# Turning the first expert item's first 256 rows: from TensorE transposes in query tiles 6 to 9 to VectorE in tiles 11 to 17

## Chip, cores, metric

One Trainium2 chip, one of its cores. The metric is device time of one execution in microseconds (us); a time of a kernel is the median of several executions.

## What is computed

Linear attention with positive random features (4 batches, 8 heads, 576 positions, head width 64, 128 features), and on its output a top-1 mixture of 8 experts over 2304 rows of 512 columns:

```python
def phi(x):                                   # x scaled by D ** -0.25
    h = x @ omega.T - sum(x * x) / 2
    return exp(h - max(h)) / sqrt(m)
q_p, k_p = phi(q), phi(k)
kv, z = k_p.T @ v, sum(k_p)                   # per batch and head
x = (q_p @ kv) / (q_p @ z + 1e-6)             # -> rows of 512
logits = x @ w_gate; e = argmax(logits)       # one expert a row, at most `capacity` rows each
out = gate * (relu(x @ w1[e]) @ w2[e])        # rows of an expert, 576 slots
```

All is float32. The expert products are made of split operands: `hi` is a value rounded to the matmul's reduced type, `lo` the rest, and hi*hi, hi*lo and lo*hi are added.

## The kernel before

The order on every engine is the order of the source: one loop (`for n in range(NK + NT + 3)`) runs over 18 groups of keys and then over query tiles, `t = n - NK`, of 128 rows. In query tile t:

- TensorE projects the queries of tile t on the features (`pjq`, L175), transposes the features of tile t - 2 (`qtr`, L782: two row halves of the array work side by side, 8 transposes each), and multiplies the transposed features of tile t - 3 with `kv_sb` into the PSUM pair `qacc` (`numer`, L654). From t = 18 on there is no projection; tiles 18 and 20 put `qacc` into other banks than the pair.
- VectorE takes the maxima `mx` of tile t's projection, half of them from PSUM (`pjq`) and half from the copy `d` (L192), and normalises tile t - 3 (`normalise`: `den`, `rec`, `xr`, `lg`, L678 to L685).
- GpSimd adds the maxima to half of `d` (L837); ScalarE does the copy, the other half and the exponentials `qpT`.
- SP's queue writes the finished rows `xr` to DRAM (`x_d`, L686) and loads queries (`load_q`, three tiles at a time, two buffers) and weights.

Beside this, generators in `tasks` advance at marks: `run("P")` lets `first_splits` do up to two steps of splitting the first item's `w1` on GpSimd (one `w1hi` of 128x1024, or one of four `w1lo` of 128x256, for each of four chunks), `run("E")` at a tile's end lets `first_item` issue a weight load. The first item (the first batch's expert) needs its 576 rows column-major, as `xhi` and `xlo`. Rows 256 to 575 are read back from `x_d` (`first_rows` in tile 15) and turned on VectorE in tiles 18 and 19 (`turn_x`, 32x32 block transposes). Rows 0 to 255 take another way: GpSimd copies the two finished tiles into `xt` (L690), TensorE transposes 64 rows in each of tiles 6 to 9 among the `qtr` (four `xtri` transposes of 64x128 a tile), ScalarE casts the result to `xhi` (L430) and VectorE subtracts to `xlo` (L432). The first expert matmul, `mm1(0, 0)`, follows `numer` in tile 20; it and the next five use rows 0 to 255 alone, then rows 256 on.

Of the kernel before, what the change touches and what calls it, by code (L numbers as in the profile page):

```python
# [19 lines left out]
B, H, S, D, M = 4, 8, 576, 64, 128  # L20
N, DM, E, FF = B * S, H * D, 8, 1024
NP = H // 2
NT = N // 128
# [13 lines left out]
AHEAD = [(0, 0)]  # L37
NJ = 11
FIRST_LOAD = 15
W1_LOADS = (0, 6, 9, 12)  # L40
W2_LOADS = 16
FIRST_AT = (6, 7, 8, 9)
BRANCH_AT = 4
EPS = 1e-6 * M
BIG = 1048576.0
# [18 lines left out]
def attention_moe(ctx, tc, kT, qT, va, om, wg, w1, w2, cap, ident, tri, desc, lst, tab0, out):  # L64
# [13 lines left out]
    def bank(i, name):  # L78
        return ps.tile([128, 512], F32, tag=f"b{i}", name=name, bufs=1)
# [68 lines left out]
    def start(gen):  # L148
        tasks.append([gen, None])
# [7 lines left out]
    def run(at=None, times=1, most=99):  # L157
        for _ in range(times):
            for task in list(tasks):
                if task[1] is None or (task[1] == at and most > 0):  # L160
                    most -= task[1] is not None
                    run_one(task)
# [9 lines left out]
    def project(parts, banks):  # L172
        def one(k, i):
            rows = slice(64 * i, 64 * i + 64)
            nc.tensor.matmul(banks[i][:, k * M : (k + 1) * M], parts[k][rows, :], om_s[rows, :], start=True, stop=True)  # L175

        a = 0
        if beside:
            a, small_t = beside.pop(0)
            small_t()  # L180
        n = len(parts)
        one(0, 1 - a)
        for k in range(1, n):
            one(k - 1, a)
            one(k, 1 - a)
        one(n - 1, a)
# [208 lines left out]
                in_offset=bass.IndirectOffsetOnAxis(ap=big["idx"][0:n, i, 2:3], axis=0),  # L395
            )

    def load_x(rows, b0=0):
        src = x_d[rows, :].rearrange("(b r) (q c) -> q r b c", r=32, q=4)
        for q in range(4):  # L400
            nc.sync.dma_start(big["xz"][32 * q : 32 * q + 32, b0:, :], src[q])


    def turn_x(b0, b1, o=0, eng=nc.vector):
        t = big["xt"][:, o : o + b1 - b0, :].rearrange("p b (k r) -> p b k r", k=4)
        nc.vector.transpose(t, big["xz"][:, b0:b1, :].rearrange("p b (a k) -> p b k a", k=4))
        t = t.rearrange("p b k r -> p k b r")
        hi, lo = (big[x][:, :, 32 * b0 : 32 * b1].rearrange("p k (b r) -> p k b r", r=32) for x in ("xhi", "xlo"))

        def split():  # L410
            nc.scalar.copy(hi, t)
            eng.tensor_tensor(lo, t, hi.bitcast(F32), op=ALU.subtract)

        return split

    def transpose_x(i, nm, at):
        n = sub_n[i]
# [186 lines left out]
    def first_item():  # L604
        yield from pause(6)
        e0 = const.tile([1, E + 2], F32, name="e0")
        e0i = const.tile([1, 1], I32, name="e0i")
        lg0 = lg[0:1, 0, :]
        nc.vector.tensor_reduce(e0[:, E : E + 1], lg0, op=ALU.max, axis=AX.X)
        yield  # L610
        nc.vector.scalar_tensor_tensor(
            e0[:, 0:E], lg0, e0[:, E : E + 1], desc_sb[0:1, :], op0=ALU.is_ge, op1=ALU.mult
        )
        yield
        nc.vector.tensor_reduce(e0[:, E + 1 : E + 2], e0[:, 0:E], op=ALU.max, axis=AX.X)
        yield
        nc.vector.tensor_scalar(e0i, e0[:, E + 1 : E + 2], -1.0, float(E), op0=ALU.mult, op1=ALU.add)
        yield
        ev = nc.sync.value_load(e0i[0:1, 0:1], min_val=0, max_val=E - 1)
        for c in range(4):  # L620
            while step[0] < W1_LOADS[c]:
                yield "E"
            load_w(1, c, ev)
            if c == 1:
                start(first_splits())
            yield "E"
        while step[0] < W2_LOADS:
            yield "E"
        for c in range(4):
            load_w(2, c, ev)  # L630
            yield "E"
# [9 lines left out]
                split_w_lo(1, c, nc.gpsimd, k)  # L641

    xr_l = {}

    def first_rows():
        load_x(slice(32 * NBA, SLOTS), NBA)
# [15 lines left out]
    def normalise(t, acc, whole):  # L664
        xr = small.tile([128, ROW, H], F32, tag="xr", name=f"xr{t}", bufs=3)
        av = [acc_i[:, 0 : NP * ROW].rearrange("p (h c) -> p c h", c=ROW) for acc_i in acc]
        if whole is not None:
            av = [whole.rearrange("p (i x) -> p i x", i=2)[:, :, 0 : NP * ROW].rearrange("p i (h c) -> p c i h", c=ROW)]
        n = len(av)
        den = small.tile([128, H], F32, tag="den", name=f"den{t}")  # L670
        rec = small.tile([128, H], F32, tag="rec", name=f"rec{t}")

        def heads(x, i, pat):
            x = x[..., i * NP : (i + 1) * NP] if n > 1 else x
            return x if n > 1 else x.rearrange(pat, i=2)

        for i in range(n):
            nc.vector.tensor_scalar(heads(den, i, "p (i h) -> p i h"), av[i][:, D], EPS, None, op0=ALU.add)  # L678
        nc.vector.reciprocal(rec, den)
        for i in range(n):  # L680
            r = heads(rec, i, "p (i h) -> p i h").unsqueeze(1)
            nc.vector.tensor_tensor(
                heads(xr, i, "p c (i h) -> p c i h"), av[i], r.to_broadcast([128, ROW, *r.shape[2:]]), op=ALU.mult
            )
        nc.vector.tensor_reduce(lg[:, t, :], xr[:, D + 1 : ROW, :], op=ALU.add, axis=AX.X)  # L685
        nc.sync.dma_start(x_d[t * 128 : (t + 1) * 128, :], xr[:, 0:D, :].rearrange("p c h -> p (c h)"))  # L686
        if t < 2:

            xr_l[t] = big["xt"][:, 4 * t : 4 * t + 4, :]
            nc.gpsimd.tensor_copy(xr_l[t], xr[:, 0:D, :].rearrange("p c h -> p (c h)").rearrange("p (m k) -> p k m", k=4))  # L690

    HALVES = [(0, 256), (256, SLOTS)]

# [42 lines left out]
    for n in range(NK + NT + 3):  # L736
# [3 lines left out]
        if n < NK:  # L740
            keys = [chunks[b, g][0][:, u * 128 : (u + 1) * 128] for b, g, u in KU[KG * n : KG * n + KG]]
            if n == 0:

                pj = [bank(i, f"pjk{n}{i}") for i in range(4)]
                project(keys[0:2], pj[0:2])
                project(keys[2:4], pj[2:4])
            else:

                if n == 1:
                    pj = [bank(SM, "pjk10"), pair("pjk11")[:, 0:512]]  # L750
                else:
                    pj = [bank(2 * (n % 2) + i, f"pjk{n}{i}") for i in range(2)]
                project(keys, pj)
        elif t < NT:
            pj = [bank((2 * t + i) % 3, f"pjq{n}{i}") for i in range(2)]
            c = max(i for i in range(len(QB) - 1) if QB[i] <= t)
            o = (t - QB[c]) * 128
            project([qc[c][:, p, o : o + 128] for p in range(NP)], pj)
        run("T")

        if 0 <= t - 2 < NT:
            d = d_l.pop(t - 2)
            trs = [bank((3 + i, (2, SM)[i])[t > NT], f"qtr{n}{i}") for i in range(2)]

            parts = [
                [(trs[i][:, u * 64 : (u + 1) * 64], d[64 * i : 64 * i + 64, u, :], i) for u in range(H)] for i in range(2)
            ]

            if t in FIRST_AT:
                k0 = FIRST_AT.index(t)  # L770
                i = k0 % 2
                tr = bank(SM, f"xtri0{k0}")
                rows = slice(64 * i, 64 * i + 64)
                x0 = xr_l[k0 // 2]
                parts[i][0:0] = [
                    (tr[:, k * 64 : (k + 1) * 64], x0[rows, k, :], i) for k in range(4)
                ]
                start(copy_x(tr, 64 * k0, 64))
            for x in chain(*zip_longest(*parts)):
                if x is not None:  # L780
                    rows = slice(64 * x[2], 64 * x[2] + 64)
                    nc.tensor.transpose(x[0], x[1], id_sb[rows, rows])  # L782
# [47 lines left out]
        else:  # L830
            if t < NT:
# [4 lines left out]
                maxima(mx, 0, d[:, 0:4, :])  # L836
                nc.gpsimd.tensor_tensor(d[:, 0:4, :], d[:, 0:4, :], spread(mx, 0), op=ALU.add)  # L837
                d_l[t] = d
            run("P", times=2, most=2)
            if 0 <= t - 2 < NT:  # L840
                qpT = qp.tile([128, 2, H * 64], F32, tag="qpT", name=f"qpT{t}", bufs=2)
                for i in range(2):
# [15 lines left out]
            if 0 <= t - 3 < NT:  # L858
                normalise(t - 3, acc_l[0], whole)
                if t == 3:  # L860
                    start(first_item())
            if t in (NT, NT + 1):

                b0 = NBA + 5 * (t - NT)
                split_x = turn_x(b0, b0 + 5, b0 - NBA, nc.gpsimd)
            run(times=3)
        if 0 <= t < NT and t - QB[c] == 2 and c + 2 < len(QB) - 1:
            load_q(c + 2)
        run("E")

        if n == NK + 1:
# [2 lines left out]
        if n < NK:  # L874

            for k in range(KB, 2 * B):
                if (9 * (k - KB) + 8) // KG + 2 == n:
                    load_k(k // 2, k % 2)
            if n == 3:
                start(setup())  # L880
            if n in (NK - 4, NK - 2):
                load_q(0 if n == NK - 4 else 1)
        if t == FIRST_LOAD:
            first_rows()
    qstack.close()
# [317 lines left out]
```

## Time and profile before

| what | value |
|---|---|
| time, median of 3 runs | 261.43 us (260.79 to 261.9) |
| the profiled execution's own time | 260.95 us |
| its span, first to last instruction | 259.2 us |
| TensorE (PE) busy | 253.7 us, 98% |
| VectorE (DVE) busy | 167.2 us, 65% |
| ScalarE (ACT) busy | 148.8 us, 57% |
| GpSimd (POOL) busy | 42.6 us, 16% |

Busy shares are means over the whole span. The key stage runs up to 46 us, the query tiles to about 101, the expert stage behind them. PE's weight loads (PEld) overlap its matmuls and stand apart. SPq is the queue from which SP issues DMAs.

### The profile page before, as it was taken

The page shows a single profiled execution, that of the slowest core. Times are in us where ns is not written, and L with a number is a line of the kernel's source. Part 1 is how long each engine was busy: PE and PEld are TensorE (multiplying, and loading weights), DVE is VectorE, ACT ScalarE, POOL GpSimd, SP SyncE. Part 2 cuts the span into 40 slices and gives each one's busy share as a digit, 9 for nine tenths or more (in the row PEclk, how much of TensorE's full clock was granted, in tenths as well). Part 3 has the DMA queues.
Part 4 walks back from the last instruction along what each step waited for, and adds up shares of the span by engine and source line. Part 5 has one row for each costly group of instructions (what it writes and reads, how often), then busy time and mean ns, then how long its engine had stood idle before and what let it go on. Part 6 is the DMA issues. An engine that isn't in the chain of part 4 may idle for free. (4 is left out here: it accounts for less than half of the span.)

```text
span 259.2 us, 7581 instructions
## 1 busy us (share of the span) xinstructions
PE 253.7 (98%) x3058; PEld 232.7 (90%) x3058; DVE 167.2 (65%) x351; ACT 148.8 (57%) x374; POOL 42.6 (16%) x61
## 2 busy tenths in 40 slices
PE   7999999999999999999999999999999999999994
PEld 6999999999999999999988789999888999998882
DVE  3999888779999998655763745566850064667500
ACT  3788888899999995326402536552361155524611
POOL 1002000255369896200000000000000000000000
PEclk9999999999999999999999999999999999999999
DMA  7999870034976769990059619992012897950121
GB/s 204 390 382 349 285 254 3 5 122 149 311 234 207 275 169 289 373 390 21 1 134 276 206 49 311 213 286 66 3 40 66 293 245 206 326 164 0 49 93 48
DMA packets 35171, 48.54 MB, mean 187 GB/s; under 512 B 2290, under 2 KB 23410, under 8 KB 35122
## 3 DMA queue, kind: packets, MB, share of 16 engines
q1 hardware_dynamic: 34002, 46.39, 57.0%
q10 hardware_dynamic: 1120, 1.52, 1.9%
q8 instruction: 28, 0.46, 0.7%
q14 instruction: 21, 0.17, 0.2%
HBM read 35.97 MB, written 11.93 MB: 185 GB/s over the span
## 5 line engine op out<-in xcount | busy, mean ns | idle before, releaser
L705 PE MATMUL hi<-xhi,w1hi 128*128 128x256 f32 (+1 forms) x192 | 56.7, 295 | 0.0
L706 PE MATMUL hi<-xhi,w1lo 128*128 128x256 f32 (+1 forms) x192 | 56.4, 294 | 0.0
L707 PE MATMUL hi<-xlo,w1hi 128*128 128x256 f32 (+1 forms) x192 | 56.3, 293 | 0.0
L718 DVE SCALAR_TENSOR_TENSOR hlo<-hi,hhi 128x256 fp32r<-128x256 f32 x48 | 20.2, 420 | 44.4 <-ACT hhi L716 22.4
L716 ACT ACTIVATE hhi<-hi 128x256 fp32r<-128x256 f32 x48 | 18.3, 384 | 36.1 <-PE hi L707 36.1
L898 PE MATMUL yi<-w2hi,hhi 128*128 128x512 f32 x96 | 37.5, 390 | 0.3 <-issue 0.3
L899 PE MATMUL yi<-w2hi,hlo 128*128 128x512 f32 x96 | 37.4, 389 | 0.0
L705 PEld LDWEIGHTS hi<-xhi,w1hi 128*128 128x128 f32 x192 | 36.0, 188 | 0.3
L706 PEld LDWEIGHTS hi<-xhi,w1lo 128*128 128x128 f32 x192 | 36.0, 188 | 0.1
L707 PEld LDWEIGHTS hi<-xlo,w1hi 128*128 128x128 f32 x192 | 36.0, 187 | 0.0
L192 DVE TENSOR_REDUCE mx<-pjk 128x4 f32<-128x512 f32 (+1 forms) x38 | 23.4, 656 | 4.2 <-PE pjk L175 4.0
L837 POOL TENSOR_TENSOR d<-d,mx 128x512 f32<-128x512 f32 x18 | 18.7, 1039 | 42.2 <-DVE mx L192 39.8
L175 PE MATMUL pjk<-om_s,kraw 64*128 64x128 f32 x288 | 23.9, 300 | 0.2
L818 ACT ACTIVATE ex<-pjk,mx 128x128 f32<-128x128 f32 x72 | 20.6, 368 | 6.0 <-DVE mx L192 5.7
L904 PE MATMUL yi<-w2lo,hhi 128*128 128x512 f32 x96 | 23.7, 389 | 0.0
L654 PE MATMUL qacc<-kv_sb,qpT 128*64 128x73 f32 x576 | 22.5, 230 | 0.1
L898 PEld LDWEIGHTS yi<-w2hi,hhi 128*128 128x128 f32 x96 | 18.0, 188 | 4.3 <-issue 0.7
L175 PEld LDWEIGHTS pjk<-om_s,kraw 64*128 64x128 f32 x288 | 20.4, 203 | 1.5 <-DMA kraw<-kT 0.6
L175 PE MATMUL pjq<-om_s,qraw 64*128 64x128 f32 x288 | 21.6, 284 | 0.0
L904 PEld LDWEIGHTS yi<-w2lo,hhi 128*128 128x128 f32 x96 | 18.0, 188 | 3.7
L899 PEld LDWEIGHTS yi<-w2hi,hlo 128*128 128x128 f32 x96 | 18.0, 188 | 3.6
L852 ACT ACTIVATE d<-pjq,mx 128x128 f32<-128x128 f32 x72 | 21.0, 404 | 0.3 <-DVE mx L192 0.3
(148 smaller groups left out, 416.4 us busy)
## 6 DMA issues: line engine op xcount, KB each, us to landing
w1raw<-w SPq DMA_DIRECT2D x16, 512.0 KB, 6.8
w2raw<-w SPq DMA_DIRECT2D x16, 512.0 KB, 5.8
qraw<-qT SPq DMA_DIRECT2D x6, 768.0 KB, 6.3
x_d<-xr SPq DMA_DIRECT2D x18, 256.0 KB, 4.3
v<-va SPq DMA_DIRECT2D x7, 650.0 KB, 6.5
xg<-x_d SPq DMA_DIRECT2D x12, 288.0 KB, 7.6
kraw<-kT SPq DMA_DIRECT2D x5, 576.0 KB, 7.0
out<-ysi SPq DMA_DIRECT2D x9, 256.0 KB, 2.1
```

The source lines that it names most:

```text
L175: nc.tensor.matmul(banks[i][:, k * M : (k + 1) * M], parts[k][rows, :], om_s[rows, :], start=True, stop=True)
L192: nc.vector.tensor_reduce(mx[:, a : a + src.shape[1]], src, op=ALU.max, axis=AX.X, negate=True)
L654: nc.tensor.matmul(acc[i][r : r + 64, p * ROW : (p + 1) * ROW], qpT[:, r // 64, (4 * i + p) * 64 : (4 * i + p) * 64 + 64], kv_sb[(t * 128 ...
L705: nc.tensor.matmul(pt, whi_[:, k, fs], xhi[:, k, sl], start=(k == 0), stop=False)
L706: nc.tensor.matmul(pt, wlo_[:, k, fs], xhi[:, k, sl], start=False, stop=False)
L707: nc.tensor.matmul(pt, whi_[:, k, fs], xlo[:, k, sl], start=False, stop=(k == 3))
L718: nc.vector.scalar_tensor_tensor(lo, src, 0.0, hi.bitcast(F32), op0=ALU.max, op1=ALU.subtract)
L818: nc.scalar.activation(ex[:, o + k, :], q[0][:, k * M : (k + 1) * M], AF.Exp, bias=mx[:, o + k : o + k + 1], scale=1.0)
L852: nc.scalar.activation(d[:, 4 + k, :], pj[1][:, k * M : (k + 1) * M], AF.Identity, bias=mx[:, 4 + k : 5 + k], scale=1.0)
L898: nc.tensor.matmul(pt, hhi[:, f, sl], w2_at(w_hi, f), start=(f == 0), stop=False)
L899: nc.tensor.matmul(pt, hlo[:, f, sl], w2_at(w_hi, f), start=False, stop=False)
L904: nc.tensor.matmul(pt, hhi[:, f, sl], w2_at(w_lo, f), start=False, stop=(f == 7))
```

## The change

Rows 0 to 255 are now read back from `x_d` at the end of tile 5 (four loads of 32 partitions x 8 blocks). In tiles 11 to 16 VectorE turns one block of 32 rows each, in tile 17 two; in tiles 12, 14, 16 and 17 GpSimd casts two blocks to `xhi` and subtracts to `xlo`. The TensorE transposes, the ScalarE casts, the VectorE subtractions and the GpSimd copies of those rows are gone. The splitting of `w1` starts when its first chunk's load is issued, not the second's, and takes one step a tile in tiles 11 to 15. A query load is issued right behind the projection that frees its buffer, not at the tile's end.

```diff
+EARLY_LOAD = 5
+EARLY = {11 + i: (i, i + 1 + (i == 6)) for i in range(7)}
-FIRST_AT = (6, 7, 8, 9)
...
+    def split_early(t):
+        b0, b1 = EARLY[t - (t < max(EARLY))][0], EARLY[t][1]
+        x = big["xt"][:, b0:b1, :].rearrange("p b (k r) -> p k b r", k=4)
+        hi, lo = (big[n][:, :, 32 * b0 : 32 * b1].rearrange("p k (b r) -> p k b r", r=32) for n in ("xhi", "xlo"))
+        split_hi(hi, x, nc.gpsimd)
+        split_lo(lo, x, hi, nc.gpsimd)
...
             load_w(1, c, ev)
-            if c == 1:
+            if c == 0:
                 start(first_splits())
...
-        if t < 2:
-            xr_l[t] = big["xt"][:, 4 * t : 4 * t + 4, :]
-            nc.gpsimd.tensor_copy(xr_l[t], xr[:, 0:D, :].rearrange("p c h -> p (c h)").rearrange("p (m k) -> p k m", k=4))
...
             project([qc[c][:, p, o : o + 128] for p in range(NP)], pj)
+            if t - QB[c] == 2 and c + 2 < len(QB) - 1:
+                load_q(c + 2)
...
-            if t in FIRST_AT:
-                k0 = FIRST_AT.index(t)
-                i = k0 % 2
-                tr = bank(SM, f"xtri0{k0}")
-                rows = slice(64 * i, 64 * i + 64)
-                x0 = xr_l[k0 // 2]
-                parts[i][0:0] = [
-                    (tr[:, k * 64 : (k + 1) * 64], x0[rows, k, :], i) for k in range(4)
-                ]
-                start(copy_x(tr, 64 * k0, 64))
...
-            run("P", times=2, most=2)
+            run("P", times=2, most=1 if 11 <= t <= 15 else 2)
...
+            if t in EARLY:
+                turn_x(*EARLY[t], EARLY[t][0])
+                if t % 2 == 0 or t == max(EARLY):
+                    split_early(t)
...
-        if 0 <= t < NT and t - QB[c] == 2 and c + 2 < len(QB) - 1:
-            load_q(c + 2)
...
+        if t == EARLY_LOAD:
+            load_x(slice(0, 32 * NBA), 0, NBA)
```

VectorE, from the maxima of tile 11 to those of tile 12 (`mx30` and `d12` are tile 12's, `den8` and `xr8` normalise tile 8). Before:

```order
L192 TENSOR_REDUCE mx29_1670<-d11_1716 128x4
L678 TENSOR_SCALAR den8_1731<-qacc11_1699 128x8
L679 RECIPROCAL rec8_1732<-den8_1731 128x8
L682 TENSOR_TENSOR xr8_1730<-qacc11_1699,rec8_1732 128x584
L685 TENSOR_REDUCE lg_86<-xr8_1730 128x8
L192 TENSOR_REDUCE mx30_1740<-pjq301_1742 128x4
L192 TENSOR_REDUCE mx30_1740<-d12_1786 128x4
```

The same place on VectorE in the changed kernel:

```order
L193 TENSOR_REDUCE mx29_1650<-d11_1698 128x4
L684 TENSOR_SCALAR den8_1712<-qacc11_1681 128x8
L685 RECIPROCAL rec8_1713<-den8_1712 128x8
L688 TENSOR_TENSOR xr8_1711<-qacc11_1681,rec8_1713 128x584
L691 TENSOR_REDUCE lg_86<-xr8_1711 128x8
L407 STREAM_TRANSPOSE xt_1008<-xg_1007 128x128
L193 TENSOR_REDUCE mx30_1720<-pjq301_1722 128x4
L193 TENSOR_REDUCE mx30_1720<-d12_1766 128x4
```

One instruction came in between `lg` and the next maxima; the same holds in tiles 12 to 16.

GpSimd, from the step on `d16` to the end of the splits (`w1hi3` and `w1lo3` are the fourth chunk of w1). Before:

```order
L837 TENSOR_TENSOR d16_2063<-d16_2063,mx34_2017 128x512
L140 TENSOR_TENSOR w1lo2_1000<-w1raw2_992,w1hi2_996 128x256
L135 TENSOR_SCALAR w1hi3_997<-w1raw3_993 128x1024
L837 TENSOR_TENSOR d17_2132<-d17_2132,mx35_2086 128x512
L140 TENSOR_TENSOR w1lo3_1001<-w1raw3_993,w1hi3_997 128x256 x4
```

The same place on GpSimd in the changed kernel:

```order
L831 TENSOR_TENSOR d16_2047<-d16_2047,mx34_2001 128x512
L136 TENSOR_SCALAR w1hi3_997<-w1raw3_993 128x1024
L141 TENSOR_TENSOR w1lo3_1001<-w1raw3_993,w1hi3_997 128x256
L136 TENSOR_SCALAR xhi_1009<-xt_1008 128x4x64
L141 TENSOR_TENSOR xlo_1010<-xt_1008,xhi_1009 128x4x64
L831 TENSOR_TENSOR d17_2119<-d17_2119,mx35_2073 128x512
L141 TENSOR_TENSOR w1lo3_1001<-w1raw3_993,w1hi3_997 128x256 x2
L136 TENSOR_SCALAR xhi_1009<-xt_1008 128x4x64
L141 TENSOR_TENSOR xlo_1010<-xt_1008,xhi_1009 128x4x64
L141 TENSOR_TENSOR w1lo3_1001<-w1raw3_993,w1hi3_997 128x256
```

Four instructions stand between d16 and d17 where two stood, and a second pair for `xhi` and `xlo` came in behind d17.

SP's queue, from the load of w1's first chunk to that of its second (`qraw3` holds the queries of tiles 9 to 11, `xr2` is tile 2's rows). Before:

```order
L376 DMA w1raw0_990<-w1 128x4x256
L686 DMA x_d_68<-xr1_1218 128x512
L686 DMA x_d_68<-xr2_1289 128x512
L209 DMA qraw3_1297<-qT 128x4x384
L686 DMA x_d_68<-xr3_1369 128x512
L376 ISA
L376 DMA w1raw1_991<-w1 128x4x256
```

The same place on SP in the changed kernel:

```order
L377 DMA w1raw0_990<-w1 128x4x256
L692 DMA x_d_68<-xr1_1217 128x512
L210 DMA qraw3_1239<-qT 128x4x384
L692 DMA x_d_68<-xr2_1289 128x512
L402 DMA xg_1007<-x_d_68 32x8x128 x4
L692 DMA x_d_68<-xr3_1366 128x512
L377 ISA
L377 DMA w1raw1_991<-w1 128x4x256
```

The query load moved one place ahead, and four loads of the finished rows stand ahead of tile 3's write and w1's second chunk.

## Rows read from the trace of the kernel before

**Rows 1.** Busy by stretch: length, PE, PEld, DVE, ACT, POOL, clock, DMA.

```profile
65.24:68.25 3.01, 3.01 (x73) 2.86 (x69) 2.73 (x8) 2.81 (x9) 0.68 (x2) 1.00 0.89 280
79.83:82.59 2.76, 2.76 (x68) 2.61 (x65) 2.54 (x6) 2.59 (x9) 2.68 (x3) 1.00 0.51 188
101.51:255.40 153.89, 153.58 (x926) 139.46 (x924) 80.96 (x164) 61.73 (x126) 3.15 (x2) 1.00 0.56 166
```

**Rows 2.** Timeline of PE's weight loads, tiles 7 and 12: start, length, instruction.

```profile
66.13 0.14 PEld L782 LDWEIGHTS xtri<-id_sb,xt 64*128 64x128 f32 x1
...
67.07 1.10 PEld L654 LDWEIGHTS qacc<-kv_sb,qpT 128*64 128x64 f32 x32
...
80.71 0.63 PEld L782 LDWEIGHTS qtr<-id_sb,d 64*128 64x128 f32 x16
81.41 1.10 PEld L654 LDWEIGHTS qacc<-kv_sb,qpT 128*64 128x64 f32 x32
```

**Rows 3.** Instructions on the tile xtri: ns min/median/max, first and last start.

```profile
L432 DVE TENSOR_TENSOR xlo<-xtri,xhi x4: 414/414/416, 64.7 to 73.9; 128x256 fp32r<-128x256 f32 x4
```

**Rows 4.** Timeline of VectorE in tile 12.

```profile
79.95 0.17 DVE L678 TENSOR_SCALAR den<-qacc 128x8 f32<-128x8 f32 x1
...
80.39 0.77 DVE L682 TENSOR_TENSOR xr<-qacc,rec 128x584 f32<-128x584 f32 x1
...
81.32 0.68 DVE L192 TENSOR_REDUCE mx<-pjq 128x4 f32<-128x512 f32 x1
81.92 0.68 DVE L192 TENSOR_REDUCE mx<-d 128x4 f32<-128x512 f32 x1
82.71 0.17 DVE L678 TENSOR_SCALAR den<-qacc 128x8 f32<-128x8 f32 x1
```

**Rows 5.** Groups by shape, line 406: count, busy us, mean ns, idle before.

```profile
L406 DVE STREAM_TRANSPOSE xt<-xg 128x1280 f32<-128x1280 f32 x3 | 7.3, 2440 | 0.0
L406 DVE STREAM_TRANSPOSE xt<-xg 128x1024 f32<-128x1024 f32 x3 | 5.9, 1980 | 5.7 <-DMA xg<-x_d 5.7
L406 DVE STREAM_TRANSPOSE xt<-xg 128x640 f32<-128x640 f32 x2 | 2.8, 1388 | 0.0
```

**Rows 6.** Timelines of VectorE and GpSimd, 98.5 to 105 us.

```profile
102.66 1.35 DVE L406 STREAM_TRANSPOSE xt<-xg 128x640 f32<-128x640 f32 x1
...
102.25 1.57 POOL L412 TENSOR_TENSOR xlo<-xt,xhi 128x640 fp32r<-128x640 f32 x1 [1.97 <-ACT xhi L411]
```

**Rows 7.** Timeline of GpSimd; in brackets the idle time before.

```profile
89.20 1.05 POOL L135 TENSOR_SCALAR w1hi<-w1raw 128x1024 fp32r<-128x1024 f32 x1
90.33 0.73 POOL L140 TENSOR_TENSOR w1lo<-w1raw,w1hi 128x256 fp32r<-128x256 f32 x1
...
93.71 1.04 POOL L837 TENSOR_TENSOR d<-d,mx 128x512 f32<-128x512 f32 x1 [0.28 <-DVE mx L192]
...
96.48 1.04 POOL L837 TENSOR_TENSOR d<-d,mx 128x512 f32<-128x512 f32 x1
97.48 2.79 POOL L140 TENSOR_TENSOR w1lo<-w1raw,w1hi 128x256 fp32r<-128x256 f32 x4
```

**Rows 8.** Timeline of PE's weight loads in tile 19, and the first expert matmul.

```profile
98.39 0.57 PEld L782 LDWEIGHTS qtr<-id_sb,d 64*128 64x128 f32 x16
...
101.51 0.19 PEld L705 LDWEIGHTS hi<-xhi,w1hi 128*128 128x128 f32 x1
```

**Rows 9.** SP's issues in time; us to landing: median of x_d, range of w1raw.

```profile
61.34 2.38 SPq L686 DMA_DIRECT2D x_d<-xr  x2
...
67.29 0.58 SPq L376 DMA_DIRECT2D w1raw<-w  x1
...
92.60 1.99 SPq L401 DMA_DIRECT2D xg<-x_d  x4
...
x_d<-xr SPq DMA_DIRECT2D x18, 256.0 KB, 4.3
...
DMA to landing us min/median/max: 4.3/6.8/10.4
```

More of the change, by code (lines that the diff above doesn't have):

```diff
@@ L396, in gather, with load_x @@
             )
-    def load_x(rows, b0=0):
+    def load_x(rows, b0=0, b1=NB):
         src = x_d[rows, :].rearrange("(b r) (q c) -> q r b c", r=32, q=4)
         for q in range(4):
-            nc.sync.dma_start(big["xz"][32 * q : 32 * q + 32, b0:, :], src[q])
+            nc.sync.dma_start(big["xz"][32 * q : 32 * q + 32, b0:b1, :], src[q])
     def turn_x(b0, b1, o=0, eng=nc.vector):
@@ L641, in first_splits @@
                 split_w_lo(1, c, nc.gpsimd, k)
-    xr_l = {}
     def first_rows():
```

## Prediction

> **What bounds the kernel now.** I read the busy time by stretch first. TensorE is busy 2.76 us of a query tile of 2.76 us, and 153.58 us of the 153.89 us from the first expert matmul to its end, at the full granted clock [rows 1]. So the time is TensorE's work. Whatever starts the expert matmuls earlier or later, at 101.51 us [rows 8], moves the end by as much; only the query tiles change here. Second, inside a tile I read TensorE's weight loads, which mark where each group of its instructions starts [rows 2]; third, VectorE's timeline in the same tile [rows 4], because two of its results come back to TensorE: `xr` frees the PSUM pair into which the next tile's `qacc` goes, and `mx` opens the way to `d` on GpSimd. VectorE is nearly full too: 2.54 us of 2.76 [rows 1]. GpSimd shows 2.68 us there, but that is w1 splitting that nobody waits for yet.
>
> **The sum, part by part.**
>
> *Transposes off TensorE.* In tile 12 the step from the first `qtr` load to the first `qacc` load is 81.41 - 80.71 = 0.70 us; in tile 7, with four `xtri` transposes among them, 67.07 - 66.13 = 0.94 [rows 2]. Four tiles carry them: 4 x 0.24 = 0.96 us saved. ScalarE's four casts and VectorE's four subtractions go as well (0.41 us each for VectorE [rows 3]). They ran beside TensorE's longer tile, and without them tile 12 already runs at TensorE's own 2.76 us, so they add nothing to the 0.96.
>
> *The turn on VectorE.* From `den` to the next `den` VectorE takes 82.71 - 79.95 = 2.76 us, TensorE's period. It could do it faster: `mx` to `mx` is 81.92 - 81.32 = 0.60, so after the second `mx` it is free at 82.52 and stands 0.19 us until `qacc` is done. Its own cycle is thus 2.57 us [rows 4]. Each of tiles 11 to 16 now adds one 128x128 STREAM_TRANSPOSE, which no row shows. From the three sizes that it does show, 640, 1024 and 1280 columns in 1388, 1980 and 2440 ns [rows 5], the bounds are: from below in proportion to the largest, 2440/10 = 0.24 us; from above by the line through the smallest and the largest (1.64 ns a column, 336 ns fixed), 0.55 us. Through 1024 and 1280 alone it is 0.37. I take 0.42, between the two lines. Back to back, an instruction of 0.68 us was followed after 0.60, so 0.08 comes off: 0.34. The cycle becomes 2.57 + 0.34 = 2.91, or 0.15 over TensorE's 2.76. Who waits: TensorE's next `qacc`, for `xr`. In tile 12 `xr` ends at 80.39 + 0.77 = 81.16 and `qacc` starts at 81.41 [rows 2, 4]; with about 0.1 for the signal, 0.15 us is spare. The turns of tiles 11 to 15 hold back `qacc` in tiles 13 to 17; tile 18's `qacc` uses other banks, so the turns of tiles 16 and 17 hold back none. That is 5 x 0.15 - 0.15 = 0.60 us given back. At 0.24 us a turn the cycle is 2.73 and nothing is given back; at 0.55 it is 3.04 and 5 x 0.28 - 0.15 = 1.25 is.
>
> [...]
>
> *Splits on GpSimd.* Most of it is covered: the w1 splitting starts three tiles earlier and is thinned to one step a tile in tiles 11 to 15, and `d` is used two tiles after it is made. The end isn't. In tile 16, between d16 and d17, GpSimd now has w1hi3, a w1lo, xhi and xlo. Start to start: d 97.48 - 96.48 = 1.00; hi 90.33 - 89.20 = 1.13; each lo 2.79/4 = 0.69 [rows 7]. The new xhi cast has 256 columns: 0.26 us in proportion to the 1.05 of 1024 columns, at most the 0.73 of a subtraction of the same size; I take 0.40 and 0.08 for its result. Together 1.00 + 1.13 + 0.69 + 0.48 + 0.69 = 3.99 us, where d17 now follows d16 after 96.48 - 93.71 = 2.77. So d17 comes 1.2 us later. It was done at 96.48 + 1.04 = 97.52 and TensorE asks for it at 98.39 [rows 7, 8]: 0.87 us of cover. That leaves a stall of 0.35 to 0.45 in tile 19. VectorE's new lateness within a tile (the 0.19 of idle time that it loses, and more) makes d16 itself up to 0.3 later against TensorE, so 0.35 to 0.75; I take 0.60. The last x split then ends about 1 us before the first expert matmul needs it; I charge nothing, and beyond that it would cost 1 for 1. The two copies that GpSimd loses in tiles 3 and 4 had nobody waiting.
>
> *DMA.* Four more loads of 128 KB go out on SP's queue, after x_d(1) has landed: 61.34 + 4.3 = 65.6 or a little more. Four issues take 1.99 us [rows 9], so they end near 67.7, and the write of tile 3 and the load of w1's second chunk, which left at 67.29, go out behind them at about 68.3. With the 4.3 to 6.8 us of such loads, least and median [rows 9] (the 10.4 is from four issued at once), it lands at 72.6 to 75.1. GpSimd asks for it in tile 8, three tiles earlier than now, and behind that wait stand d9 and then TensorE's transposes of d9 in tile 11: 80.71 - 2.76 = 77.95 now, and 77.0 with the 0.96 saved. Back from there, less 0.1 for the signal, 1.04 for d9 and 1.0 for w1hi1, the load must have landed by 74.8. I charge nothing, at 73.5, and keep the other end as a rival. The query loads now go out right behind the projection that frees their buffer, ahead of that tile's write; nothing waited for them before, so that gains nothing by itself, but keeps them in time when tiles come sooner.
>
> Sum: -0.96 + 0.60 + 0.60 = +0.24 us. On the profiled execution's 260.95 us that is 261.2; on the median of the runs, 261.43, which is 0.48 above it, 261.7. I say **261.5 us**, no measurable change: 0.5% is 1.3 us, about what a measurement of this kernel can tell from no change.
>
> **The rivals.**
>
> *The saving stays* (20%). If a turn costs 0.30 us or less and xhi 0.3, VectorE's cycle fits into 2.8 and the stall at d17 is near 0.35: -0.96 + 0.35 = -0.6, and at the very best -0.96: 260.5 to 260.8. For it speaks the slope between the larger turns; against it, that small VectorE instructions don't shrink in proportion (128x4x64 takes 0.41 us [rows 3]).
>
> *w1's second chunk comes late* (13%; the other side). From a landing at 74.8 us on, each microsecond is one that TensorE waits in tile 11 and that GpSimd carries to d17: at 76, +1.2 on the sum, 262.9. For it: 512 KB of new traffic and a later issue, ahead of the same load. Against it: the query load ahead has left earlier, and another load of this size took 4.3.
>
> *A turn is held by GpSimd* (4%). GpSimd is busy most of each of these tiles; if a turn had to wait for the instruction that GpSimd is in, some 0.5 us on average, the cycle would be 3.4 and 5 x 0.65 - 0.15 = 3.1 given back: +2.8 on the sum with 0.7 at d17, 264.2. The rows speak against it: the turn at 102.66 lies wholly beside a GpSimd subtraction (102.25 to 103.82) and takes 1.35 us, no longer than the group's mean [rows 5, 6]. [...]
>
> *Turns and casts at their upper ends* (8%): -0.96 + 1.25 + 0.8 = +1.1, 262.4.
>
> **How the numbers follow.** My case, a net change between -0.4 and +1.0, has 55%: 260.9 to 262.3. With the saving kept below (260.5) and the upper ends and the late chunk above (262.4, 262.9), and the spread of a median of three (260.79 to 261.9 before), the range is 260.2 to 263.0. Faster by over 0.5% needs more than the whole saving, or luck: 0.07. Slower by over 0.5%, above 262.7: most of the late chunk and the held turn, and some of the upper ends: 0.17. The same: 0.76.
>
> **What would show it.** Right: tiles 6 to 10 all at 2.76 us; tiles 13 to 17 at 2.9, with VectorE without a gap and `qacc` starting right after `xr`; a gap of some half microsecond before the transposes of tile 19, ended by GpSimd's d17; STREAM_TRANSPOSE 128x128 near 0.42 us; expert matmuls starting within 0.8 us of 101.5. Wrong: tiles 12 to 17 still at 2.76 (turns too cheap to matter), a wait in tile 11 for d9 behind w1hi1's DMA, turns much longer than 0.55, or a first expert matmul that waits for `xlo`.

## Result, and the profile after

The changed kernel takes 263.04 us (median of 22 runs, 261.08 to 264.28), the kernel before 261.21 (22 runs, 260.08 to 263.15): ratio 1.0065, interval 1.0047 to 1.0082. It is slower by some 1.7 us. The forecast was no measurable change, 261.5 us; the median lies 0.04 above the top of its range, and 0.65% is above the 0.5% that was to count as slower, though the interval reaches down to 0.47%. The profiled execution takes 263.24 us, span 261.5.

The first expert matmul starts at 103.27 us, where it was 101.51 [rows 8]; the expert stage is no longer than it was. So that loss arises in the query tiles. (The two profiled executions differ by 2.29 us. Another 0.73 lies behind the last matmul, where the end takes 3.82 us before and 4.55 after; e6 and e10, one kernel, take 3.78 and 4.04 there, so I don't put it down to the change.) The stretches: length, then PE, PEld, DVE, ACT, POOL busy (instructions), granted clock, DMA share, GB/s. The first two are tiles 6 and 9, the third is tile 14.

```profile
62.03:64.99 2.96, 2.96 (x75) 2.87 (x72) 2.66 (x7) 2.63 (x8) 1.16 (x2) 1.00 0.90 260
71.44:74.20 2.76, 2.76 (x67) 2.61 (x65) 2.54 (x6) 2.60 (x9) 1.66 (x2) 1.00 1.01 331
85.25:89.04 3.79, 3.12 (x67) 2.79 (x64) 3.39 (x8) 2.63 (x9) 2.34 (x4) 1.00 0.71 237
103.27:256.95 153.68, 153.64 (x926) 139.56 (x924) 80.59 (x163) 61.15 (x126) 3.23 (x3) 1.00 0.56 164
```

Tiles 7 and 9 to 13 run at 2.76 us, or 0.01 above, as forecast; tile 6 takes 2.96, because it has eight weight loads of `wg_sb` besides (0.32 us from 64.64 on), as it had before. But TensorE now stands still three times. The view of its waits over 62 to 104 us, which is empty for the kernel before, gives total, times, longest; "issue" means that it waited for nothing that the profile names:

```profile
PE pjq L176 <- issue: 1.3, 2, 0.7
PE qtr L776 <- POOL d L831: 0.7, 1, 0.7
```

The timeline of weight loads shows where: in tile 8 behind the 12th load of the projection, in tile 14 behind the 5th, and in tile 19 ahead of the transposes. In brackets stands the idle time before a row.

```profile
67.76 0.75 PEld L176 LDWEIGHTS pjq<-om_s,qraw 64*128 64x128 f32 x12
69.34 0.30 PEld L176 LDWEIGHTS pjq<-om_s,qraw 64*128 64x128 f32 x4 [0.84 <-issue]
...
85.25 0.41 PEld L176 LDWEIGHTS pjq<-om_s,qraw 64*128 64x128 f32 x5
86.51 0.63 PEld L176 LDWEIGHTS pjq<-om_s,qraw 64*128 64x128 f32 x10 [0.86 <-issue]
...
98.21 1.10 PEld L660 LDWEIGHTS qacc<-kv_sb,qpT 128*64 128x64 f32 x32
100.16 0.58 PEld L776 LDWEIGHTS qtr<-id_sb,d 64*128 64x128 f32 x16 [0.84 <-POOL d L831]
...
103.27 0.19 PEld L707 LDWEIGHTS hi<-xhi,w1hi 128*128 128x128 f32 x1
```

Tile 8 takes 3.68 us and tile 14 takes 3.79. Each stop comes in the middle of a projection, though the matmuls ahead of it read the same query tile and write the same two banks. The account against before, by the starts of the tiles: tiles 6 to 9 take 0.09 less (1.01 saved on the transposes, 0.92 given back in tile 8), tiles 10 to 13 the same, tiles 14 to 16 take 1.10 more (1.03 in tile 14, 0.07 in tile 16), and from tile 17 to the first expert matmul 0.77 more (the wait of 0.70 for d17 among them). That is +1.77.

What stands near the unnamed stops is a packet of the instruction queue. Its rows by window (packets, MB, share of 16 engines): from 63.2 to 66.9 us there is none on q8, while the packets of q1, the queue of data, take 102.9%; then, in the next 0.1 us, there is one. It begins at 66.91 and takes 1.03.

```profile
q1 hardware_dynamic: 964, 1.33, 102.9%
...
q1 hardware_dynamic: 24, 0.04, 96.9%
q8 instruction: 1, 0.02, 64.6%
```

The packet holds 16,384 bytes. It ends 1.40 us before TensorE goes on in tile 8; the next such pair is 84.11 to 85.09, then 1.42 us to 86.51. Between the two stops the trace records 768 instructions of TensorE, those of its sequencer among them: 3 x 256, and 16,384 / 256 is 64 bytes for one. The first instruction behind either stop has, in the trace's list of TensorE's instructions, counted from 0, number 193 plus a multiple of 256 (2753 and 3521). I call these places boundaries. From the boundary at 63.15 us to the one at 103.05 q8 has exactly one packet between each two, and so it has before, from 63.16 to 100.77. It begins 2.21 to 4.04 us behind its boundary in the changed kernel (seven packets, 66.91 to 99.66), before 0.42 to 2.48 (seven, 65.05 to 98.21). So I take it that a packet holds a block of 256 instructions, that the one between two boundaries holds the block behind the second, and that it is asked for at the first. That is my reading of these places and times: no trace shows what a packet holds, nor a request.

Ahead of each of the two packets a query load of 768 KB had gone out, at 62.03 and at 78.76, and TensorE passed the boundary before, where by this reading the block is asked for, 1.12 and 1.30 us later. Counted by their size of 1,536 bytes, 472 of the first load's 512 packets had started before the block did, and 488 of the second's. That was the theory to test: the earlier query loads get in front of TensorE's own instructions. Rivals: an operand or a bank that the trace doesn't name; the early x loads; plain shortage of transfer.

### The profile page after: what moved, and what is told of

Read it like the earlier page. It is cut to its first block, busy times and chain, and to the rows that moved or that the text cites. A ratio compares the mean times of both kernels' runs of the same rounds, so it can differ in the third digit from the quotient of the medians.

```text
span 261.5 us, 7560 instructions
## 1 busy us (share of the span) xinstructions
PE 253.2 (97%) x3042; PEld 231.9 (89%) x3042; DVE 168.3 (64%) x354; ACT 147.6 (56%) x370; POOL 44.6 (17%) x67
## 3 DMA queue, kind: packets, MB, share of 16 engines
q10 hardware_dynamic: 1120, 1.52, 1.9%
## 5 line engine op out<-in xcount | busy, mean ns | idle before, releaser
L176 PE MATMUL pjq<-om_s,qraw 64*128 64x128 f32 x288 | 22.3, 285 | 1.3 <-issue 1.3
L407 DVE STREAM_TRANSPOSE xt<-xg 128x128 f32<-128x128 f32 (+4 forms) x15 | 19.1, 1276 | 5.4 <-DMA xg<-x_d 5.4
```

## Experiments

Executions differ by over a microsecond ahead of the query tiles, where nothing was changed (the first query tile starts at 46.10 us in the changed kernel, at 45.63 in e8 and at 47.25 in e11). So besides the time I read, in each profile, the time from the start of tile 6 to the first expert matmul: 39.47 us before, 41.25 in the changed kernel (differences of rounded times, good to 0.01). Ratios are to the kernel before, with their intervals.

| kernel | time, us | ratio | tile 6 to expert, us |
|---|---|---|---|
| e1 queries back | 263.32 | 1.0096 (1.0058 to 1.0133) | 41.90 |
| e2 split early | 261.35 | 1.0012 (0.9988 to 1.0036) | 40.13 |
| e3 pad of 64 | 263.03 | 1.0080 (1.0052 to 1.0107) | 41.15 |
| e4 = e1 + e2 | 261.74 | 1.0022 (1.0001 to 1.0043) | 40.59 |
| e5 = e2 + query pairs | 260.56 | 0.9994 (0.9963 to 1.0026) | 39.13 |
| e6 move alone, on before | 260.57 | 0.9996 (0.9969 to 1.0023) | 39.43 |
| e7 = e5, turns twice | 264.02 | 1.0109 (1.0049 to 1.0170) | 41.86 |
| e8 change again | 262.46, one run | | 41.15 |
| e9 x loads late | 262.43 | 1.0062 (1.0020 to 1.0104) | 40.06 |
| e10 = e6 again | 261.12, one run | | 39.43 |
| e11 pad of 16 | 263.06 | 1.0057 (1.0032 to 1.0082) | 41.09 |
| e12 = e5, x loads late | 260.18 | 0.9980 (0.9955 to 1.0005) | 39.97 |

**e3, instructions moved.** The 16 transposes of tile 4 are done three times over:

```diff
-            for x in chain(*zip_longest(*parts)):
+            for x in chain(*zip_longest(*parts), *(zip_longest(*parts) if t == 4 else ()), *(zip_longest(*parts) if t == 4 else ())):
```

> The change with the 16 transposes of tile 4 done three times over (same operands, same result): 64 more TensorE instructions, some 1.3 us, ahead of tile 5, nothing else moved. Instruction-block theory: every boundary of 256 instructions falls 64 instructions earlier in the program. The block is then asked for some 1.4 us earlier against the query load, just about when that load is issued, so the two gaps leave their places (after the 12th and the 10th matmul of the projections of tiles 8 and 14); a gap that stays stands 64 instructions further ahead, in tiles 7 and 13. Time 263.2 to 264.6, with both gaps gone 263.0. Operand theory: both gaps stay after the same matmuls of tiles 8 and 14, all times 1.3 us later: 264.3 to 264.6.

(By the loads alone, the stop in tile 14 comes behind the 5th matmul, not the 10th.) No stop in tile 8 nor in tile 7. The other is now in tile 13, behind the 5th weight load of `qacc`:

```profile
84.29 0.26 PEld L660 LDWEIGHTS qacc<-kv_sb,qpT 128*64 128x64 f32 x5
85.61 0.96 PEld L660 LDWEIGHTS qacc<-kv_sb,qpT 128*64 128x64 f32 x27 [1.07 <-issue]
```

From there to the old place are the 27 loads left of `qacc` and 5 of the projection: 32 pairs of load and matmul, exactly the 64 instructions put in. A third stop, 0.36 us, is new in tile 11, again ended 1.5 us after a packet of q8 (landed 77.50). A stop that keeps its distance in instructions and not its place among the operands is a matter of the instructions themselves. The operand theory falls. The count says the same in all the profiles: every stop of over 0.3 us without a named releaser in these tiles (the changed kernel, e2, e3, e8, e11, e12) ends at a boundary, at number 193 plus a multiple of 256.

**e1, the query loads back at the tile's end.**

```diff
-            if t - QB[c] == 2 and c + 2 < len(QB) - 1:
-                load_q(c + 2)
         run("T")
...
+        if 0 <= t < NT and t - QB[c] == 2 and c + 2 < len(QB) - 1:
+            load_q(c + 2)
         run("E")
```

> The change with one part undone: the query loads go out at the end of their tile again, some 2 us later. Instruction-block theory: in the changed kernel TensorE stood 0.65 us in tile 8 (68.70) and 0.66 us in tile 14 (85.85), 768 recorded instructions (3 x 256) apart, because a 16 KB packet of the instruction queue began only at 66.9 and 84.1, behind a query load of 768 KB issued at 62.03 and 78.76; each landed 1.4 us before TensorE went on. With the loads back, both gaps are gone and these two tiles give back 0.92 and 1.04 us; VectorE's turns, whose lateness the stop in tile 14 had swallowed, then cost 0.1 to 0.4 in tiles 15 to 17. First expert matmul at 101.4 to 101.8 us in place of 103.27, time 261.2 to 261.8. Operand theory (TensorE waits in these tiles for a bank or for data, not for instructions): the gaps stay after the same matmul, time 262.8 to 263.3.

Half of it came: both unnamed stops are gone. The time didn't follow, since now the queries themselves are late, in tiles 9 and 15:

```profile
PE pjq L176 <- DMA qraw<-qT: 1.8, 2, 0.9
PE qtr L774 <- POOL d L829: 0.7, 1, 0.7
```

So the move was needed: without it TensorE waits 0.88 and 0.94 us for `qraw`, with it 0.65 and 0.66 for instructions.

**e2, w1's last hi cast ahead of d16.**

```diff
-            run("P", times=2, most=1 if 11 <= t <= 15 else 2)
+            run("P", times=2, most=1 if t in (11, 12, 13, 14, 16) else 2)
```

> The change with w1's last hi cast put on GpSimd ahead of d16 (into the 1.11 us in which GpSimd waited there), not between d16 and d17. GpSimd theory: d17 is then made about 1.0 us earlier, the gap of 0.69 us before the transposes of tile 19 is gone, first expert matmul at 102.5 to 102.7 us, time 262.2 to 262.6. The gaps in tiles 8 and 14 stay as they are. Rival: something else is late in tile 19 as well (VectorE's last turns), and 0.3 us or more of the gap stays: 262.6 to 263.0.

In the changed kernel GpSimd stood 1.11 us before d16 and then did hi, lo, xhi and xlo before d17:

```profile
95.06 1.04 POOL L831 TENSOR_TENSOR d<-d,mx 128x512 f32<-128x512 f32 x1 [1.11 <-DVE den L684]
96.06 1.04 POOL L136 TENSOR_SCALAR w1hi<-w1raw 128x1024 fp32r<-128x1024 f32 x1
97.19 0.73 POOL L141 TENSOR_TENSOR w1lo<-w1raw,w1hi 128x256 fp32r<-128x256 f32 x1
97.89 0.40 POOL L136 TENSOR_SCALAR xhi<-xt 128x256 fp32r<-128x256 f32 x1
98.38 0.73 POOL L141 TENSOR_TENSOR xlo<-xt,xhi 128x256 fp32r<-128x256 f32 x1
99.06 1.04 POOL L831 TENSOR_TENSOR d<-d,mx 128x512 f32<-128x512 f32 x1
```

With the cast in that idle time, tile 19's transposes follow without a wait:

```profile
98.32 1.10 PEld L660 LDWEIGHTS qacc<-kv_sb,qpT 128*64 128x64 f32 x32
99.50 0.58 PEld L776 LDWEIGHTS qtr<-id_sb,d 64*128 64x128 f32 x16
```

Better than expected: 261.35 us, not measurably slower than before. In the profile tile 14 also lost only 0.23 us, tile 8 as much as ever (3.84). e8 says why that is not the edit's doing.

**e8, the change again.**

> The changed kernel once more, for a second profile. If the gaps in tiles 8 and 14 come from where the instructions and the loads stand in the program, both are there again, after the same matmuls, 0.4 to 1.1 us each; if they were chance, one or both are gone and the first expert matmul comes at 101.9 to 102.6 us.

Tile 8 stops once more (3.84 us), tile 14 takes 2.97 in place of 3.79, tile 10 takes 3.25, tile 19 waits 0.79 for d17. The stop in tile 8 is thus in all three profiles with this order of loads; the second one varies in size and place.

**e4, e1 and e2 together.**

> The two edits of e1 and e2 together. If the gaps in tiles 8 and 14 and the one in tile 19 are each what the theories say, their gains add: first expert matmul 100.7 to 101.2 us, time 260.5 to 261.1, up to 0.25% below the kernel before. If one swallows the other (a stop in tile 14 gives GpSimd and VectorE time to catch up, so that without it more waits show later): 261.1 to 261.8.

The wait at d17 is gone, but tile 9 waits 1.46 us for queries, so the gains don't add: 261.74 us lies in the second range, though it is the queries that take the gain. With no stop behind tile 9, VectorE's turn shows at last. Tiles 13 to 16 take 2.80, 2.86, 2.87 and 2.86 us, VectorE's own cycle from `den` to `den`, without idle time:

```profile
86.14 0.15 DVE L684 TENSOR_SCALAR den<-qacc 128x8 f32<-128x8 f32 x1
...
87.50 0.42 DVE L407 STREAM_TRANSPOSE xt<-xg 128x128 f32<-128x128 f32 x1
...
89.01 0.14 DVE L684 TENSOR_SCALAR den<-qacc 128x8 f32<-128x8 f32 x1
```

**e6 and e10, the move alone.** In the kernel before, `load_q` is put where the change has it, and nothing else.

```diff
             project([qc[c][:, p, o : o + 128] for p in range(NP)], pj)
+            if t - QB[c] == 2 and c + 2 < len(QB) - 1:
+                load_q(c + 2)
...
-        if 0 <= t < NT and t - QB[c] == 2 and c + 2 < len(QB) - 1:
-            load_q(c + 2)
```

> The kernel before with one part of the change alone: the query loads go out right behind the projection. The prediction charged nothing for it. Instruction-block theory: the load behind tile 5 goes out at 62.0 and the block of instructions is asked for at 63.2, so it lands near 68.0 in place of 65.9; the boundary is passed at 68.5, so a gap of 0.5 to 0.9 us appears in tile 8, labelled issue. Behind tile 11 the load (79.9) follows the request (79.4): no gap in tile 14. First expert matmul at 102.0 to 102.4 us, time 261.7 to 262.1. Rival (the move is harmless, the early x loads are what makes the blocks late): no gap, 261.0 to 261.4.

> e6 (the move of the query loads alone, in the kernel before) for a second profile. In e6 the block was asked for 1.11 us behind the query load's issue and got ahead of its packets; in the changed kernel, 1.12 us behind, it came after them. If that is an edge on which the order falls by chance, this profile may show the gap of 0.5 to 0.9 us in tile 8 and 40.0 to 40.4 us from tile 6 to the first expert matmul; if it is fixed by the program, no gap again and 39.4.

The rival was right: no stop in either profile. In e6 the block begins at 64.43, when only 7 of the 512 packets of the query load issued at 61.55 had started (8 in e10). The window from 64.4 to 64.5:

```profile
q1 hardware_dynamic: 29, 0.04, 106.4%
q8 instruction: 1, 0.02, 54.9%
```

So an earlier query load by itself doesn't delay the block, and my theory of its cause was too simple.

**e9, the early x loads behind tile 8.**

```diff
-EARLY_LOAD = 5
+EARLY_LOAD = 8
```

> The change with its early x loads (4 x 128 KB) behind tile 8 and not behind tile 5. e6 had shown no gap with the query loads moved alone, so something else of the change must hold the block of instructions for tile 8 back. If it is the x loads' 512 KB: the block begins near 64.9 in place of 66.9, no gap in tile 8, from the start of tile 6 to the first expert matmul 40.1 to 40.5 us in place of 41.25. If it is the place of the block's request behind the query load alone (the x loads go out at 65.9, after the block of e6 was already under way): gap of 0.6 to 0.9 us in tile 8 as in the changed kernel, 41.0 to 41.4.

The block for tile 8 begins at 65.47, and there is no unnamed stop in any query tile. What is left is d17, as the prediction had foreseen, and VectorE:

```profile
PE qtr L776 <- POOL d L831: 0.8, 1, 0.8
PE qacc L660 <- DVE xr L688: 0.4, 1, 0.4
```

VectorE's wait is in part new: the x loads now go out at 72.68 us, so the first turn, in tile 11, comes late, and the wait of 0.4 us for `xr` in tile 13 follows from it:

```profile
81.15 0.43 DVE L407 STREAM_TRANSPOSE xt<-xg 128x128 f32<-128x128 f32 x1 [0.34 <-DMA xg<-x_d]
```

The profile gains 1.2 us on the changed kernel; the ratio (1.0062, where the changed kernel has 1.0065) doesn't show that gain.

**e11, a pad of 16 instructions.**

```diff
-            for x in chain(*zip_longest(*parts)):
+            again = list(zip_longest(*parts))[4:8] if t == 4 else []
+            for x in chain(*zip_longest(*parts), *again):
```

> The change with 8 of the transposes of tile 4 done once more: 16 TensorE instructions, some 0.33 us, ahead of tile 5. Every block of 256 is then asked for 16 instructions, about 0.35 us, earlier against the query loads: 0.77 us behind the one issued at the end of tile 5 (1.12 in the changed kernel), 0.95 behind that of tile 11 (1.30). If the order of the two requests decides, within about a microsecond of each other: both blocks get ahead of the query load's packets, no gap in tiles 8 and 14, from tile 6 to the first expert matmul 39.5 to 40.0 us. If not: gaps as in the changed kernel, 16 instructions further ahead, 41.0 to 41.4.

For tile 8 it held: with early x loads and moved queries both in place, the block asked for 0.95 us behind the query load begins 1.25 us later (3.76 in the changed kernel) and nothing stops. But in this execution the issue of the four x loads took 3.15 us in place of 2.40, w1's second chunk went out 8.7 us after the start of tile 6 (63.37) in place of 7.0, and the prediction's rival came in: d9 behind the late cast, TensorE behind d9 in tile 11, so that the next boundary came 1.83 us behind a query load and not 0.95; its block began 3.58 us later, and TensorE stopped for 0.42 us in tile 13. The profiled execution, 264.14 us, is the slowest of the kernel's ten (median 263.06), so the others need not have had all of this.

```profile
77.23 1.05 POOL L136 TENSOR_SCALAR w1hi<-w1raw 128x1024 fp32r<-128x1024 f32 x1 [3.58 <-DMA w1raw<-w]
78.24 1.04 POOL L832 TENSOR_TENSOR d<-d,mx 128x512 f32<-128x512 f32 x1
...
79.33 0.58 PEld L777 LDWEIGHTS qtr<-id_sb,d 64*128 64x128 f32 x16 [0.99 <-POOL d L832]
```

**e5, e7 and e12, queries in pairs of tiles.** On e2's order:

```diff
-QT = 3
-QB = [0, 3, 6, 9, 12, 15, 18]
+QT = 2
+QB = [0, 1, 3, 5, 7, 9, 11, 13, 15, 17, 18]
...
-        raw = qp.tile([128, NP, QT * 128], F32, tag="qraw", name=f"qraw{c}")
+        raw = qp.tile([128, NP, QT * 128], F32, tag="qraw", name=f"qraw{c}", bufs=3)
...
-            if t - QB[c] == 2 and c + 2 < len(QB) - 1:
-                load_q(c + 2)
+            if t + 1 == QB[c + 1] and c + 3 < len(QB) - 1:
+                load_q(c + 3)
...
+            if n == NK - 2:
+                load_q(2)
```

> e2 with the queries loaded in chunks of two tiles into three buffers (512 KB a load) in place of three tiles into two (768 KB): the same memory, one tile more between a load and its use, and every load goes out at the start of an odd tile, while TensorE passes its boundaries of 256 instructions in even tiles, 1.1 us after their start; so a block is asked for some 3.9 us after a query load and not 1.1. Instruction-block theory: no gap in tiles 8 and 14, no wait for queries in tiles 9 and 15 either; what is left of the changed kernel's loss is VectorE's 2.87 us cycle in tiles 13 to 17, 0.3 to 0.5 us. First expert matmul at 100.8 to 101.2 us, time 260.5 to 261.0. Rival, plain shortage of transfer: the same bytes move, so blocks or queries come late elsewhere, a gap of 0.5 us or more remains in tiles 6 to 17, time 261.3 to 262.

No stop for instructions and none for queries, time within the range. Not all of the rest is VectorE's: tile 11 takes 3.10 us, since GpSimd's cast of w1's second chunk waited until 75.00 (2.90 us idle, ended by the DMA of `w1raw`). Against before, the pieces stand at -1.0 for the transposes, +0.34 in tile 11 and +0.35 in tiles 13 to 16; the time is the same as before.

e7 calls `turn_x` twice in each of tiles 11 to 17:

> e5 with each turn done twice (same operands, same result). If VectorE's cycle sets the pace of tiles 13 to 17, each further turn of 0.34 us net comes on top: den to den 3.2 us, five tiles at about 3.2, +1.6 to +1.9 us against e5, 262.2 to 262.8. If turns lie in time that nobody waits for: less than +0.5 against e5.

Tiles 13 to 16 take 3.26, 3.32, 3.33 and 3.32 us, 0.46 more than in e5 for one more turn, and TensorE waits for `xr` (the views give five waits of up to 0.5):

```profile
PE qacc L660 <- DVE xr L688: 2.4, 5, 0.5
PE qtr L776 <- POOL d L831: 0.4, 2, 0.2
```

VectorE does set the pace of these tiles. The price was higher than expected (2.7 us more from tile 6 to the first expert matmul, 3.5 on e5's time): a second turn costs 0.46, not 0.34, and d is late behind VectorE as well.

e12 is e5 with `EARLY_LOAD = 7`:

> e5 with the early x loads behind tile 7 and not behind tile 5, so that w1's second chunk goes out ahead of them. In e5 GpSimd's cast of that chunk waited until 75.00 us (landed 74.93), d9 came behind it, and tile 11 took 3.10 us in place of 2.76. Theory: the chunk lands near 72, tile 11 takes 2.76, nothing else moves, and from tile 6 to the first expert matmul it takes 38.7 to 38.9 us (39.13 in e5, 39.47 in the kernel before): time 260.0 to 260.5, 0.1 to 0.3% below the kernel before. Rival: the x loads now collide with a query load or a block of instructions of tiles 8 to 12, and a wait of 0.3 us or more shows there: 39.1 to 39.8 us, time as before or slower.

Tile 11 is back at 2.76, but its profile has a stop for instructions in tile 14 (0.54 us) and one near 100.6 (0.35): the rival. The time, 260.18 us, is the lowest of all; its ratio to before is not told apart from 1.

## Why the prediction was right or wrong

The terms of the sum came out right or a little high. The time came out at the very top of the range all the same, in the profile 1.5 us above the sum, by a cost that stands in no term. That it isn't higher still is in part luck: the stops hid the cost of the turn and covered w1's late second chunk.

*Transposes, -0.96:* right. 0.24 in tiles 6 and 7, 1.01 in all.

*The turn, +0.60:* the mechanism was right, the size a little high, and in the changed kernel the term is absent. A turn takes 416 ns (0.42 taken), VectorE's cycle is 2.87 us (2.91 taken), and in e4, where nothing else stops TensorE, tiles 13 to 16 lose 0.04, 0.10, 0.11 and 0.10 and tile 17 some 0.07 (nearly the same in e5); e7 shows that TensorE follows VectorE there. In the changed kernel the stop in tile 14 let VectorE catch up: it then stood 0.30 us until `qacc` was done, ahead of `den` at 89.16. The 0.07 of tile 16 is not the turn's: it arises in the projection, whose second matmul starts 0.17 us later than in tile 15, and `xr` had been done 0.23 us before `qacc` (93.22 and 93.45). So tiles 12, 13 and 15 at 2.76 us, a sign of "turns too cheap to matter", came about although the turns were as dear as forecast. The 0.1 us taken for a signal stands in no row; in the changed kernel `d` starts 0.08 us after the `mx` that it waited for (62.24 to 88.94 us, five waits) and TensorE's transposes of tile 19 0.05 after d17. The group by shape: count, busy us, mean ns.

```profile
L407 DVE STREAM_TRANSPOSE xt<-xg 128x128 f32<-128x128 f32 x6 | 2.5, 416 | 0.0
```

That no turn is held by GpSimd is borne out by these six: each begins while GpSimd is in an instruction, four of them (84.08, 86.96, 93.39 and 96.26 us) lie wholly within one, and they take 0.41 to 0.43 us with no idle time before them. So the half microsecond that this rival adds to a turn shows nowhere. One reading against it was wrong, though: the turn at 102.66 did not lie wholly beside GpSimd's subtraction but ended at 104.01, 0.19 us after it.

*Splits, +0.60:* right; 0.70 and 0.79 us in two profiles, and e2 takes it away. d17 follows d16 after 4.00 us, where the sum had 3.99.

*w1's second chunk, nothing:* nothing was lost, but by luck. In the changed kernel's profile the cast started at 74.60 us, 0.2 inside the bound of 74.8. In the second profile of the same kernel (e8) it started at 75.70, some 7.0 us after the load's issue at 68.58 where 6.8 was the most taken, and tile 11 didn't wait because the stop in tile 8 had put TensorE itself off by 1.08 us. (The 10.4 set aside as from four loads issued at once is from the first of four issued over 6 us, at 163.23 to 169.13.) In e5 (75.00, with tiles 0.2 us earlier and no stop) and e11 (77.23, with tiles 1.3 us later) tile 11 waited.

*The query loads and the x loads:* this is the step that failed. The part on DMA charged the new x loads only with w1's chunk, and of the query loads it says "that gains nothing by itself, but keeps them in time". In time they were (e1 shows the 1.8 us of waiting that the move saves). What the sum left out is what else moves as packets beside these loads: q8, the instruction queue, has 28 packets of 16,384 bytes in the changed kernel, among them, as I read it, TensorE's own instructions. There two of these blocks came late and cost 0.92 us in tile 8 and 1.03 in tile 14. This 1.95, with the 0.07 in tile 16 and less the 0.60 that the turns then didn't cost, is 1.42; with 0.17 more from tile 17 on than the 0.60 forecast, and 0.05 more saved on the transposes, it is 1.54, which is to rounding the difference between +0.24 and +1.77.

The figures of the range stand on two bases: 260.9 to 262.3 and 262.4 on the 261.5 of the forecast, 260.5, 262.9 and 264.2 on the 261.43 of before. On that one the first three would be 0.17 higher.

What makes the blocks late is shown in part: the late ones in tile 8 come behind nearly all of a query load. Where TensorE stopped in tile 8, 472, 493 and 485 of the load's 512 packets had started before the block (the changed kernel, e8, e2); at the same place, or 16 or 64 instructions ahead of it, where it didn't stop, 7, 8, 18, none and 20 (e6, e10, e9, e11, e3). It is not for want of transfer in general: in the changed kernel and in e9 the load's first packet starts 1.52 and 1.53 us after the boundary, with no x load issued in either, and only then do the two part. A query load is not the only thing that can do it: near 100.6 us e12 stops with none ahead of the block; what it waited behind stays open.

What decides which goes first was not found. For tile 8's block it takes both edits: with the query loads back (e1, e4), with the x loads elsewhere (e9), or with neither the x loads nor the rest of the change (e6, e10), the block begins 1.7 to 1.9 us after the boundary, and in the three profiles with both 3.75 to 3.76. A shift of 16 or 64 instructions cures this one as well (e11, e3), but not the next, in tile 13. The x loads went out at 65.9 us, after the time at which the block would have begun, so they can't have stood in front of it by themselves. Nor is it the time between the two requests, as I place them: a block asked for 1.10 to 1.11 us behind the query load was in time (e6, e10, e9) and one 1.12 behind was late, which a sharp edge would fit, but in e3 one that was asked for 0.62 us behind began 4.10 us later. That stays open.

## What to carry to other kernels

Look in the profile for waits labelled issue at equal distances in instructions (here multiples of 256), and for a packet of the instruction queue that ends shortly before each wait is over (here 1.29 to 1.54 us). In the changed kernel, with q1 at 102.9% from 63.2 to 66.9 us, such a packet began 3.76 us behind its boundary, and tile 8 lost 0.92 us. Making tiles shorter brings forward every deadline: here the saving of 1 us moved the limit from TensorE to loads that had had 0.1 us to spare (tile 9's queries landed at 71.2 in the kernel before, and tile 9 began at 71.3). And two late things in one place can hide each other: the turn's cost appeared only when the stops were gone.

## What the runs showed of the hardware that was not expected

Such a stop cost more than its gap: with gaps of 0.65 and 0.66 us, tiles 8 and 14 lost 0.92 and 1.03, and with one of 0.54 tile 14 of e12 lost 0.81. Where a block came late, TensorE went on 1.29 to 1.54 us after the block had landed (stops of over 0.3 us in the changed kernel, e2, e3, e8, e11 and e12), so by these figures, as an estimate, a block that lands a microsecond ahead of its boundary is already late. A STREAM_TRANSPOSE of 128x128 f32 took 416 ns and one of 128x256 took 630; GpSimd's cast of 128x256 took 405 ns where 128x1024 took 1047.
